# Attention in plain fp32 on part tiles of the array instead of three-way splits, with a new plan

## The chip, the cores and the metric

The kernel runs on one core of a Trainium2 chip. The metric is device microseconds of one execution; lower is better. The engines are TensorE (PE, with its weight loads shown apart as PEld), VectorE (DVE), ScalarE (ACT), GpSimd (POOL) and SyncE (SP), which issues most DMAs.

## The reference

Block attention, then a mixture of experts (two of eight per token), then a gated two-layer network. The change lies in the attention alone, with `q`, `k`, `v` of 4 batches, 8 heads, 576 tokens and 64 features in fp32:

```python
block = 64
scores = (1.0 / np.sqrt(D)) * np.matmul(q, k.transpose(0, 1, 3, 2))
mask = block_i >= block_j                  # a block of 64 queries sees its own and earlier blocks
scores = np.where(mask, scores, -1000000000.0)
scores = scores - np.max(scores, axis=-1, keepdims=True)
attn = np.exp(scores)
attn = attn / (np.sum(attn, axis=-1, keepdims=True) + 1e-09)
attn_out = np.matmul(attn, v)
```

The result, 2304 tokens by 512, is the input of the experts.

## The kernel before

The attention goes through 16 pairs of heads (4 batches, 4 pairs each). `q` and `k` arrive with the features of two heads on the 128 partitions; a query block `i` (of 9, `NB`) needs the keys of blocks 0 to `i`, so `L = 64 (i + 1)` columns. For a pair the stages are: scores (L789), row maximum on DVE (L797), exponential with row sum on ACT (L803), transposes of the 128x128 parts of P on PE (L815), copies out of PSUM (L686), P times V (L847), a closing matmul with `iw` (L871), which is an identity with the router's columns beside it, so that it turns the result back and forms router logits at once, and a scaling by the inverse row sums (L878).

Matmuls are done in three parts of a reduced fp32 format (`F32R`): each operand is split into a high part (a rounding copy) and a low part (the rest), and high x high, high x low and low x high are added up in PSUM. The splits are `hi` and `lo` for V (POOL L749), `q_hi` and `q_lo` (L686, L762), `k_hi` and `k_lo` (L690, L772), and `pt_hi` and `pt_lo` for P (L686, L836). The scores of both heads come from one matmul: `qd` holds a query block of both heads in block-diagonal form, 128x128 with zeros off the diagonal. PV uses a stationary tile of V's high and low part side by side (128 columns), one head at a time. The closing matmul and the transposes run in plain fp32. After each batch three small matmuls with `half` (L894 to L896) add the logits of the two heads.

PSUM has 8 banks: five for transposes, PV and closing results (`tb`), and three for the scores (`sb`, of one and of two).

The order of all this is set by a planner, `Plan`. Each operation is added with the engines that can run it and their costs, with what it depends on, and with a priority; the planner goes through time and, on each free engine, starts the ready operation with the lowest number. `PR` holds the priorities, `TURN` the planner's charge for a change of kind on PE, `STICK` its preference to stay with a kind, `SLACK` how long it waits for the first engine of a choice. The instructions are then issued in that order. DMAs that bring `q`, `k`, `v` of the next pairs and four pairs of expert weights (`RAWP`) are operations of SP in the same plan. Behind the attention come a second plan for the start of the first expert, with tokens known before the last batch is routed, and then written-out loops for the experts and the last network.

Of the kernel before, what the change touches and what calls it, by code (L numbers as in the profile page):

```python
# [7 lines left out]
F32 = mybir.dt.float32  # L8
# [6 lines left out]
OP = mybir.AluOpType  # L15
# [18 lines left out]
SLACK = 0.58  # L34
# [5 lines left out]
STICK = 2.77  # L40
TURN = {(a, b): t for b, r in {"S": {"T": 0.045, "V": 0.083, "F": 0.086, None: 0.084}, "V": {"T": 0.134, "S": 0.072, "F": 0.086, None: 0.09},
                               "T": {"V": 0.038}}.items() for a, t in r.items()}
# [4 lines left out]
PR = {'last': -75, 'ranks': 30, 'rows': -100.0, 'hold': 0.1, 'na': 185.6, 'nb': 352.4, 'lsel': (0, 0, 0, 0, 0, 0, 0, 1, 0, 0), 'f1': (1.7, 24.4, 76.4, 3.2, -11.4, -24.0, -70.7, 4.7), 'f2': (49.7, 0.7, 5.8, 6.0, 38.9, 4.0, 76.2, -1.1), 'fa': (31.8, 1.5, 49.4, -13.5), 'fb': (-32.0, -64.8, 88.3, 44.5), 'fh': (-0.9, 2.5, -24.8, -10.3, 69.9, -36.6, 9.5, -21.3), 'fl': (-24.5, 48.5, -15.0, -13.5, -2.8, 11.5, -62.3, -104.3), 'v': -317.22, 'qk': -13.33, 'keep': 1, 'S': -2.19, 'max': -82.24, 'exp': -40.31, 'pt': 0.29, 'hi': 360.75, 'lo': -37.22, 'hid': True, 'av': 7.35, 'o': 252.33, 'od': True, 'inv': 36.95, 'fin': 28.78, 'x': -1.53, 'route': -0.9, 'rp': 1, 'route2': 6.36, 'xt': -459.1, 'eg': 587.2, 'ex': 432.13, 'ew': 2149.25, 'first': 0, 'sel': 2, 'vh': 3, 'wl': 1, 'wa': -452.8, 'wb': 26.5, 'h': -53.9, 's2': -24.9, 'vs': (-0.62, -2.53, 0.92, 0.17, 0.59, -5.66), 'vpt': (28.74, 8.73, -37.77, -2.51, -5.17, 6.9, -0.23, 1.96), 'vp': (-2.81, -6.08), 'vf': (15.46, 3.5)}  # L47
# [139 lines left out]
def kernel(  # L187
# [49 lines left out]
    FIRST = ((0, 4 * BLK), (4 * BLK, S))  # L237
# [23 lines left out]
    qd = [[raw_p.tile([128, NB, 2, BLK], F32R, name=f"qd{i}{w}") for w in "hl"] for i in range(2)]  # L261

    def zero_qd(e, i):
        for t in qd[i]:
            for h in range(2):
                e.memset(t[64 * h:64 * h + 64, :, 1 - h].bitcast(F32), 0.0)

    zero_qd(nc.vector, 0)
# [15 lines left out]
    FW = D + 4 * E  # L284
    iw = raw_p.tile([128, NP2, FW], F32, name="iw")

    def setup():
        zero_qd(nc.vector, 1)
        for r in range(2):
            rows = slice(r * 64, (r + 1) * 64)  # L290
            nc.vector.tensor_copy(iw[rows, :, 0:D], ident[rows, None, r * 64:(r + 1) * 64].to_broadcast([64, NP2, D]))
# [373 lines left out]
    with actx:  # L665
        pool = lambda name, bufs: actx.enter_context(tc.tile_pool(name=name, bufs=bufs))
        one = pool("one", 1)
        sp_p = pool("split", 3)
        qk_p = pool("qk", 2)
        sm_p = pool("sm", 10)  # L670
        ps_p = actx.enter_context(tc.tile_pool(name="ps_p", bufs=1, space=PSUM))
# [6 lines left out]

        UN = ((0, 1, 3), (2, 4), (5,), (6,), (7,), (8,))
        NU = len(UN)  # L680
        NPAIR = len(pairs)
        BW = 5 * 128
        PART = ((0, 4), (4, NB))
# [3 lines left out]

        def scale(e, o, i):
            if e == "ACT":
                nc.scalar.mul(o, i, qscale)  # L690
            else:
                nc.vector.tensor_scalar(o, i, qscale, None, op0=OP.mult)
# [10 lines left out]
        def first_dve(n):  # L703
            return {"DVE": 0.07 + n / 960.0, "ACT": 0.05 + n / 1200.0}

        def dve(n):
            return {"DVE": 0.07 + n / 960.0}

# [4 lines left out]
        nc.gpsimd.memset(eps, 1.0e-9)  # L713
        P = []
        for i in range(NB):
            P.append(one.tile([128, (i // 2 + 1) * 128], F32, name=f"P{i}"))
            if i % 2 == 0:
                nc.gpsimd.memset(P[i][:, (i + 1) * BLK:], 0.0)
        rs = [one.tile([128, NB], F32, name=f"rs{i}") for i in range(3)]
        pt = [[one.tile([128, 4, 2, 128], F32R, name=f"pt{w}0"), one.tile([128, 5, 5, 128], F32R, name=f"pt{w}1")]  # L720
              for w in "hl"]
        half = one.tile([128, 192], F32, name="half")
        nc.gpsimd.memset(half, 0.0)
        for r in range(2):
            nc.gpsimd.tensor_copy(half[r * 64:(r + 1) * 64, 64:128], ident[r * 64:(r + 1) * 64, r * 64:(r + 1) * 64])
        lgp = [one.tile([128, NB, 2 * E], F32, name=f"lgp{i}") for i in range(2)]

        def init_iw(e):
            for r in range(2):
                rows = slice(r * 64, (r + 1) * 64)  # L730
                for i in range(2):
                    for j, src in enumerate((w_gate, w_noise)):
                        o = D + i * 2 * E + j * E
                        nc.sync.dma_start(iw[rows, :, o:o + E], src.rearrange("(j i d) e -> i d j e", d=D, i=2)[i])
# [4 lines left out]
        sp, kt, oT, ri, xt = {}, {}, {}, {}, {}  # L739

        def hi(e, p):
            t = sp_p.tile([128, NC * 2, 2, D], F32R, tag="v", name="sp_v")
            copy(e, t[:, :, 0], raw["v", p % 2].rearrange("p c h d -> p (c h) d"))
            sp[p] = t

        def lo(e, p):
            t = sp[p]
            r = raw["v", p % 2].rearrange("p c h d -> p (c h) d")
            engine(e).tensor_tensor(t[:, :, 1], r, t[:, :, 0].bitcast(F32), op=OP.subtract)  # L749
            sp[p] = t.rearrange("p (c h) w d -> p c h (w d)", h=2)  # L750

        def rows(t, r, c):
            return t[r, c[0]:c[1]].rearrange("p (i s) -> p i s", s=BLK)

        def q_hi(e, p, h, c=(0, S)):
            r = slice(64 * h, 64 * h + 64)
            copy(e, qd[p % 2][0][r, c[0] // BLK:c[1] // BLK, h], rows(raw["q", p % 2], r, c))

        def q_lo(e, p, h, c=(0, S)):
            r = slice(64 * h, 64 * h + 64)  # L760
            i = slice(c[0] // BLK, c[1] // BLK)
            engine(e).tensor_tensor(qd[p % 2][1][r, i, h], rows(raw["q", p % 2], r, c),  # L762
                                    qd[p % 2][0][r, i, h].bitcast(F32), op=OP.subtract)

        def k_hi(e, p, c=(0, S)):
            if p not in kt:
                kt[p] = [qk_p.tile([128, S], F32R, tag=nm, name=nm) for nm in ("kh", "kl")]
            scale(e, kt[p][0][:, c[0]:c[1]], raw["k", p % 2][:, c[0]:c[1]])

        def k_lo(e, p, c=(0, S)):  # L770
            sl = slice(*c)
            nc.vector.scalar_tensor_tensor(kt[p][1][:, sl], raw["k", p % 2][:, sl], qscale, kt[p][0][:, sl].bitcast(F32),  # L772
                                           op0=OP.mult, op1=OP.subtract)

        views = {}

        def scores(p, u):
            ps = sb[u % 2]
            o = 0
            qh, ql = [t.rearrange("p i h s -> p i (h s)") for t in qd[p % 2]]  # L780
            kh, kl = kt[p]
            for i in UN[u]:
                L = (i + 1) * BLK
                nh = 1 if L <= 512 else 2
                hl = L // nh
                for half_ in range(nh):
                    ks_ = slice(half_ * hl, (half_ + 1) * hl)
                    for a, (w, x) in enumerate(((qh, kh), (qh, kl), (ql, kh))):
                        nc.tensor.matmul(ps[:, half_, o:o + hl], lhsT=w[:, i], rhs=x[:, ks_], start=(a == 0), stop=(a == 2))  # L789
                views[p, i] = ps[:, 0, o:o + hl] if nh == 1 else ps[:, :, :hl]  # L790
                o += hl
# [3 lines left out]
        def rowmax(p, i):  # L795
            nm = sm_p.tile([128, 1], F32, tag="nm", name="nm")
            nc.vector.tensor_reduce(nm, views[p, i], axis=AX.X if i < NB - 1 else AX.XY, op=OP.max, negate=True)  # L797
            nms[p, i] = nm

        def expo(p, i):  # L800
            L = (i + 1) * BLK
            o = P[i][:, :L] if i < NB - 1 else P[i][:, :L].rearrange("p (a l) -> p a l", a=2)
            nc.scalar.activation(o, views.pop((p, i)), AF.Exp, bias=nms.pop((p, i)), scale=1.0,  # L803
                                 accum_out=rs[p % 3][:, i:i + 1])

# [6 lines left out]
        def ptrans(g, n):  # L812
            ps = tb[g.bank]
            for m, (i, c) in enumerate(PT[n]):
                nc.tensor.transpose(ps[:, m * 128:(m + 1) * 128], P[i][:, c * 128:(c + 1) * 128], ident)  # L815

        def pslice(w, n):
            i0, c0 = PT[n][0]
            i1, c1 = PT[n][-1]
            if i1 < 4:  # L820
                return pt[w][0][:, i0:i1 + 1, c0:c1 + 1]
            return pt[w][1][:, i0 - 4, c0:c1 + 1]

        def pview(g, n):
            i0, c0 = PT[n][0]
# [790 lines left out]
```

## Time and profile before

| | |
|---|---|
| median of 3 runs | 1065.29 us (1065.21 to 1066.15) |
| the profiled execution | 1067.7 us, of which its span is 1065.9 us |
| PE busy | 1052.2 us, 99% of the span |
| DVE, ACT, POOL busy | 775.7, 593.3, 319.2 us |
| attention's matmuls | from 5.09 to 227.69 us |
| granted clock, mean | 0.994 |

A matmul's time in the trace is from its start to the modelled end of its result, so successive matmuls overlap in the trace; how often one can start is read from the starts. `128*128` in a row is the size of the stationary tile, `128x320` that of the moving one. A plain fp32 instruction stands in the trace as two records.

### The profile page before, as it was taken

To read this page: it belongs to the slowest core of one execution; us is meant where nothing else is said; L and a number is where in the kernel's file an instruction comes from. 1 tells how busy PE (TensorE), PEld (TensorE's weight loads), DVE (VectorE), ACT (ScalarE), POOL (GpSimd) and SP (SyncE) were. 2 spreads that over 40 slices of the span, in tenths; PEclk is the share of its full clock that TensorE was granted. 3 is DMA by queue.
4 is the path that set the end of the run, shared out by engine and by line. 5 is a ranking of instruction groups with operands and counts; after the bars stand their busy time and mean duration, and the time that the engine had idled before them with its cause. 6 is when DMAs were issued, how large, how long until landed. Compare 5 with 4: busy or idle time off the path is not lost. (4 is left out here: it accounts for less than half of the span.)

```text
span 1065.9 us, 16930 instructions
## 1 busy us (share of the span) xinstructions
PE 1052.2 (99%) x6069; PEld 924.7 (87%) x6069; DVE 775.7 (73%) x1469; ACT 593.3 (56%) x1121; POOL 319.2 (30%) x380
## 2 busy tenths in 40 slices
PE   8999999999999999999999999999999999999998
PEld 6999999988888999999888898988888888888886
DVE  8878787877688889988787866775745755665442
ACT  5777777764456655656555535664535444454442
POOL 6558787624101121202020002743401411310000
PEclk8999999999999999999999999999999999999999
DMA  7534432024999999987978425222202211201001
GB/s 186 147 97 126 132 87 60 16 52 134 323 289 330 281 302 306 264 243 232 218 235 216 155 69 200 78 60 60 60 1 70 51 40 49 60 10 40 1 1 40
DMA packets 163573, 141.80 MB, mean 133 GB/s; under 512 B 92373, under 2 KB 131381, under 8 KB 163485
## 3 DMA queue, kind: packets, MB, share of 16 engines
q1 hardware_dynamic: 147501, 102.79, 35.1%
q0 software_dynamic: 8640, 28.32, 8.9%
q10 hardware_dynamic: 7344, 9.57, 2.7%
q8 instruction: 49, 0.80, 0.3%
q14 instruction: 39, 0.32, 0.1%
HBM read 92.94 MB, written 36.70 MB: 122 GB/s over the span
## 5 line engine op out<-in xcount | busy, mean ns | idle before, releaser
L464 PE MATMUL h<-xh,wah 128*128 128x512 f32 (+8 forms) x832 | 273.3, 328 | 0.7 <-ACT xh L435 0.7
L465 PE MATMUL h<-xl,wah 128*128 128x512 f32 (+8 forms) x832 | 271.9, 327 | 0.4 <-DVE xl L440 0.3
L466 PE MATMUL h<-xh,wal 128*128 128x512 f32 (+8 forms) x832 | 272.0, 327 | 0.0
L1168 PE MATMUL y<-wbl,hh 128*128 128x512 f32 (+1 forms) x576 | 225.7, 392 | 0.1
L1167 PE MATMUL y<-wbh,hh 128*128 128x512 f32 (+1 forms) x576 | 225.6, 392 | 0.1
L1169 PE MATMUL y<-wbh,hl 128*128 128x512 f32 (+1 forms) x576 | 225.0, 391 | 0.0
L464 PEld LDWEIGHTS h<-xh,wah 128*128 128x128 f32 x832 | 156.8, 189 | 16.0 <-ACT xh L435 0.9
L465 PEld LDWEIGHTS h<-xl,wah 128*128 128x128 f32 x832 | 157.0, 189 | 15.5 <-DVE xl L440 0.9
L466 PEld LDWEIGHTS h<-xh,wal 128*128 128x128 f32 x832 | 156.9, 189 | 11.5
L1169 PEld LDWEIGHTS y<-wbh,hl 128*128 128x128 f32 (+1 forms) x576 | 107.3, 186 | 24.7
L487 ACT ACTIVATE hh<-h 128x288 fp32r<-128x288 f32 (+7 forms) x128 | 53.1, 417 | 131.5 <-PE h L466 130.8
L1168 PEld LDWEIGHTS y<-wbl,hh 128*128 128x128 f32 (+1 forms) x576 | 107.4, 186 | 21.4 <-POOL wbl L419 0.8
L1167 PEld LDWEIGHTS y<-wbh,hh 128*128 128x128 f32 (+1 forms) x576 | 107.4, 186 | 21.2 <-issue 0.6
L1530 DVE SCALAR_TENSOR_TENSOR r<-r,h 128x512 f32<-128x512 f32 (+1 forms) x80 | 50.5, 631 | 97.9 <-ACT r L1529 97.6
L1529 ACT ACTIVATE r<-h,three 128x512 f32<-128x512 f32 (+1 forms) x80 | 51.7, 646 | 118.8 <-PE h L466 118.8
L419 DVE TENSOR_TENSOR wal<-wa,wah 128x1024 fp32r<-128x1024 f32 x80 | 106.2, 1328 | 11.8 <-ACT wah L415 10.8
L419 DVE TENSOR_TENSOR wbl<-wb,wbh 128x1024 fp32r<-128x1024 f32 x75 | 101.3, 1350 | 14.8 <-ACT wbh L415 14.6
L415 ACT CAST wbh<-wb 128x1024 fp32r<-128x1024 f32 x80 | 83.9, 1048 | 24.5 <-PE y L1169 14.5
L1532 ACT CAST hh<-r 128x512 fp32r<-128x512 f32 (+1 forms) x80 | 46.2, 577 | 86.0 <-DVE r L1530 86.0
L1533 DVE TENSOR_TENSOR hl<-r,hh 128x512 fp32r<-128x512 f32 (+1 forms) x80 | 56.4, 705 | 51.5 <-ACT hh L1532 51.5
L803 ACT ACTIVATE P<-sb,nm 128x192 f32<-128x192 f32 (+4 forms) x144 | 74.8, 529 | 28.8 <-DVE nm L797 28.8
L415 ACT CAST wah<-wa 128x1024 fp32r<-128x1024 f32 x80 | 83.7, 1046 | 3.9 <-PE h L465 2.4
(269 smaller groups left out, 1785.9 us busy)
## 6 DMA issues: line engine op xcount, KB each, us to landing
wa<-in_moe_w_dram SPq DMA_DIRECT2D x23, 512.0 KB, 4.9
wb<-in_moe_w_dram SPq DMA_DIRECT2D x23, 512.0 KB, 5.6
y_tab<-yo SPq DMA_DIRECT2D x32, 256.0 KB, 4.8
w<-in_moe_w_in_dram SPq DMA_DIRECT2D x16, 512.0 KB, 5.2
y_tab<-zero SPq DMA_DIRECT2D x8, 1024.0 KB, 9.2
w<-in_moe_w_out_dram SPq DMA_DIRECT2D x16, 512.0 KB, 5.6
x_tok<-x SPq DMA_DIRECT2D x32, 144.0 KB, 2.6
wa<-in_moe_w_dram ACTq DMA_DIRECT2D x9, 512.0 KB, 6.3
```

The source lines that it names most:

```text
L415: nc.scalar.copy(w_s[which, u][0], raws[PS[u]][which])
L419: (nc.gpsimd if e == "POOL" else nc.vector).tensor_tensor(lo, raws[PS[u]][which], hi.bitcast(F32), op=OP.subtract)
L464: nc.tensor.matmul(ps, lhsT=wh, rhs=xh, start=first, stop=False)
L465: nc.tensor.matmul(ps, lhsT=wh, rhs=xl, start=False, stop=False)
L466: nc.tensor.matmul(ps, lhsT=wl, rhs=xh, start=False, stop=last)
L487: nc.scalar.activation(h[0][:, c0:c1], ps[:, :c1 - c0], AF.Relu)
L803: nc.scalar.activation(o, views.pop((p, i)), AF.Exp, bias=nms.pop((p, i)), scale=1.0, accum_out=rs[p % 3][:, i:i + 1])
L1167: nc.tensor.matmul(yps[t][:n], lhsT=hh[:, sl], rhs=wh[:, f % 2], start=first, stop=False)
L1168: nc.tensor.matmul(yps[t][:n], lhsT=hh[:, sl], rhs=wl[:, f % 2], start=False, stop=False)
L1169: nc.tensor.matmul(yps[t][:n], lhsT=hl[:, sl], rhs=wh[:, f % 2], start=False, stop=last)
L1529: nc.scalar.activation(r[:, :n], ps[:, :n], AF.Relu, bias=three, scale=1.0)
L1533: nc.vector.tensor_tensor(hl[:, :n], r[:, :n], hh[:, :n].bitcast(F32), op=OP.subtract)
```

## The change

Scores, PV and the closing matmul become plain fp32 matmuls, and the splits of `q`, `k`, `P` and `V` go; only `q` is scaled once (`q_scale`, POOL). Scores are done for each head by itself with 64 partitions and 64 columns of the array: of an odd block and of block 0 head 0 uses the first half of rows and of columns and head 1 the second half of both, and of the other even blocks the columns are exchanged (`flip`). PV and the closing matmul use 128 rows and 64 columns, head 0 (or token half 0) in the first half of the columns. The closing result comes out in token order, so router logits of both heads lie on the same partitions and are added on POOL; the matmuls with `half` go. Scores take four banks, transposes and the rest four. The scores of a pair are three units instead of six: blocks 0 to 4, 5 and 6, 7 and 8. All priorities of the attention's plan are new.

```diff
-SLACK = 0.58
+SLACK = 0.13684749096082838
-STICK = 2.77
+STICK = 3.1977009815403736
+TURN = {(a, b): 0.155 if a and b else 0.09 for a in ("S", "T", "V", None) for b in ("S", "T", "V", None) if a != b}
-        NTB = 5
+        NTB = 4
-        sb = [ps_p.tile([128, i + 1, 512], F32, name=f"sb{i}") for i in range(2)]
+        sb = [ps_p.tile([128, n, 512], F32, name=f"sb{i}") for i, n in enumerate((2, 2))]
-        UN = ((0, 1, 3), (2, 4), (5,), (6,), (7,), (8,))
+        UN = ((0, 1, 2, 3, 4), (5, 6), (7, 8))
+        SAT = {0: (0, 0, 0), 1: (0, 0, 64), 3: (0, 0, 192), 2: (0, 1, 0), 4: (0, 1, 192), 5: (1, 0, 0), 6: (1, 1, 0),
+               7: (1, 0, 0), 8: (0, 0, 0)}
+        ORDER = ((0, 2, 1, 3, 4), (5, 6), (7, 8))
+        SPOOL = ("s0", "s1", "s0")
+        SCOST = (0.87, 0.77, 0.98)
-        PART = ((0, 4), (4, NB))
+        PART = ((0, 5), (5, NB))
+        TPART = ((0, 3), (3, NC))
+        def flip(i):
+            return int(i > 0 and i % 2 == 0)
...
+        def sview(i):
+            t, n, o = SAT[i]
+            L = (i + 1) * BLK
+            return sb[t][:, n, o:o + L] if i < NB - 1 else sb[t][:, 0:2, 0:L // 2]
         def scores(p, u):
-            for i in UN[u]:
+            q_, k_ = qs[p % 2], raw["k", p % 2]
+            for i in ORDER[u]:
...
-                    for a, (w, x) in enumerate(((qh, kh), (qh, kl), (ql, kh))):
-                        nc.tensor.matmul(ps[:, half_, o:o + hl], lhsT=w[:, i], rhs=x[:, ks_], start=(a == 0), stop=(a == 2))
+                for m in range(nh):
+                    for h in range(2):
+                        r = slice(64 * h, 64 * h + 64)
+                        g = h ^ flip(i)
+                        o = sview(i)[64 * g:64 * g + 64]
+                        nc.tensor.matmul(o if nh == 1 else o[:, m], lhsT=q_[r, i * BLK:(i + 1) * BLK],
+                                         rhs=k_[r, m * w:(m + 1) * w], start=True, stop=True)
...
-        def av(g, p, h, part):
+        def av(g, p, part):
...
+            todo = [(c, r) for c in range(last + 1) for r in runs(max(i0, 2 * c), i1)]
+            for n, (c, (a, b)) in enumerate(todo):
+                for h in range(2):
...
+                    nc.tensor.matmul(o[64 * h:64 * h + 64, (a - i0) * BLK:(b - i0) * BLK], lhsT=vs[:, c, h], rhs=x,
+                                     start=(n == 0), stop=(n == len(todo) - 1), skip_group_check=True)
...
         def fin(g, p, part):
-            for i in range(i1 - i0):
-                nc.tensor.matmul(f[:, i], lhsT=oT[p, part][:, i].rearrange("p h s -> p (h s)"), rhs=iw[:, p % NP2],
-                                 start=True, stop=True)
+            for c in range(*TPART[part]):
+                for r in range(2):
+                    i = 2 * c - 1 + r if c else 0
+                    x = oT[p, part][:, (i - i0) * BLK:(i - i0 + 1) * BLK] if c or not r else none
+                    nc.tensor.matmul(f[64 * r:64 * r + 64, c - TPART[part][0]].rearrange("p h w -> p (h w)"), lhsT=x, rhs=w,
+                                     start=True, stop=True)
...
-                k["S", p, u] = add({"PE": sum(s_cost(i) for i in UN[u])}, lambda e, p=p, u=u: scores(p, u),
-                                   ready, U + PR["S"], take=g, kind="S")
+                k["S", p, u] = add({"PE": SCOST[u]}, lambda e, p=p, u=u: scores(p, u),
+                                   ready[0] + (ready[-1] if u else []) + ([k["E", p, 5]] if u == 2 else [k.get(("E", p - 1, 7))] if u == 1 else []), U + PR["S"], take=g, kind="S",
+                                   after=LAND[min(u, 1)] + 0.1 if p == 0 else 0.0)
```

On PE, the scores of three small blocks of a pair before: for each block high x high, low x high and high x low (`kh`, `kl` are the parts of k, `qd1h`, `qd1l` those of q), on the whole array.

```order
L789 MATMUL sb_173<-kh,qd1h 128x64
L789 MATMUL sb_173<-kl,qd1h 128x64
L789 MATMUL sb_173<-kh,qd1l 128x64
L789 MATMUL sb_173<-kh,qd1h 128x128
L789 MATMUL sb_173<-kl,qd1h 128x128
L789 MATMUL sb_173<-kh,qd1l 128x128
L789 MATMUL sb_173<-kh,qd1h 128x256
L789 MATMUL sb_173<-kl,qd1h 128x256
L789 MATMUL sb_173<-kh,qd1l 128x256
```

The same place in the changed program: seven blocks of a pair in one run, and the transposes behind them. `x2` is one matmul for each head.

```order
L752 MATMUL sb_164<-raw_k_77,qs_87 64x64 x2
L752 MATMUL sb_164<-raw_k_77,qs_87 64x192 x2
L752 MATMUL sb_164<-raw_k_77,qs_87 64x128 x2
L752 MATMUL sb_164<-raw_k_77,qs_87 64x256 x2
L752 MATMUL sb_164<-raw_k_77,qs_87 64x320 x2
L752 MATMUL sb_165<-raw_k_77,qs_87 64x384 x2
L752 MATMUL sb_165<-raw_k_77,qs_87 64x448 x2
L777 MATMUL tb_160<-ident,P_0_196 128x128
```

Three matmuls a block for both heads have become two, one a head, and two units of scores stand together.

On PE, the end of the large PV part of one head and the small parts of both heads before (`pth`, `ptl` are the parts of the transposed P).

```order
L847 MATMUL tb_172<-pth_197,sp_v 128x192
L847 MATMUL tb_172<-ptl_199,sp_v 64x192
L847 MATMUL tb_172<-ptl_199,sp_v 64x64
L847 MATMUL tb_172<-pth_197,sp_v 128x64
L847 MATMUL tb_168<-pth_196,sp_v 128x256
L847 MATMUL tb_168<-ptl_198,sp_v 128x256
L847 MATMUL tb_168<-ptl_198,sp_v 64x128
L847 MATMUL tb_168<-pth_196,sp_v 128x128
```

The changed program from the closing matmuls of one part over the large PV part of the next pair to the last scores and the transposes behind.

```order
L857 MATMUL tb_162<-iw,oT_696 64x160
L857 MATMUL tb_162<-iw,none 64x160
L857 MATMUL tb_162<-iw,oT_696 64x160 x4
L822 MATMUL tb_160<-pt_867,raw_v_72 64x256 x6
L822 MATMUL tb_160<-pt_867,raw_v_72 64x64 x2
L822 MATMUL tb_160<-pt_867,raw_v_72 64x128 x2
...
L752 MATMUL sb_165<-raw_k_77,qs_87 64x512 x2
L752 MATMUL sb_164<-raw_k_77,qs_87 64x288 x4
L777 MATMUL tb_161<-ident,P_1_185 128x128 x3
```

Both heads of PV now stand in one run with one bank, and PE goes from column halves to quadrants to the whole array within these rows.

On ACT, one pair before, from the exponentials of blocks 2 and 4 to those of 0, 1 and 3, with copies of P's high part between them.

```order
L803 ACTIVATE P_182,rs_194<-sb_174,nm 128x192
L803 ACTIVATE P_185,rs_194<-sb_174,nm 128x320
L686 CAST pth_197<-tb_168 128x512
L803 ACTIVATE P_179,rs_194<-sb_173,nm 128x64
L803 ACTIVATE P_181,rs_194<-sb_173,nm 128x128
L803 ACTIVATE P_184,rs_194<-sb_173,nm 128x256
L686 CAST pth_196<-tb_171 128x2x128
```

The same place in the changed program: the exponentials of the five small blocks (`P_0_184` is block 4) with the copies of the transposed P of other blocks between them.

```order
L766 ACTIVATE P_0_172,rs_200<-sb_164,nm 128x64
L766 ACTIVATE P_0_176,rs_200<-sb_164,nm 128x128
L685 COPY pt_1023<-tb_160 128x128
L766 ACTIVATE P_0_178,rs_200<-sb_164,nm 128x192
L766 ACTIVATE P_0_182,rs_200<-sb_164,nm 128x256
L685 COPY pt_1023<-tb_163 128x512
L685 COPY pt_1136<-tb_162 128x2x128
L766 ACTIVATE P_0_184,rs_200<-sb_164,nm 128x320
L766 ACTIVATE P_0_188,rs_200<-sb_165,nm 128x384
```

All five share the banks of `sb_164`, which the scores of block 8 take next.

## Rows read from the trace of the kernel before

**Rows 1.** The page: span, busy time of each engine, and slices.

```profile
span 1065.9 us, 16930 instructions
...
PE 1052.2 (99%) x6069; PEld 924.7 (87%) x6069; DVE 775.7 (73%) x1469; ACT 593.3 (56%) x1121; POOL 319.2 (30%) x380
...
PE   8999999999999999999999999999999999999998
...
PEclk8999999999999999999999999999999999999999
```

**Rows 2.** Stages: length, busy PE, PEld, DVE, ACT, POOL, clock, DMA, GB/s.

```profile
12.00:25.00 13.00, 11.45 (x58) 10.47 (x59) 11.61 (x23) 7.92 (x24) 10.59 (x12) 0.61 0.61 154
...
38.00:51.00 13.00, 13.00 (x106) 12.58 (x104) 10.77 (x24) 10.20 (x32) 6.88 (x7) 1.00 0.55 153
...
90.00:103.00 13.00, 12.75 (x106) 12.30 (x105) 11.94 (x44) 9.81 (x32) 8.64 (x15) 1.00 0.47 130
```

**Rows 3.** PE in order of time (start, length), at the attention's two ends.

```profile
5.09 0.38 PE L789 MATMUL sb<-kh,qd0h 128*128 128x64 f32 x1
...
30.74 0.45 PE L789 MATMUL sb<-kh,qd1h 128*128 128x448 f32 x1
...
215.67 0.45 PE L789 MATMUL sb<-kh,qd1h 128*128 128x448 f32 x1
...
225.62 2.23 PE L871 MATMUL tb<-iw,oT 128*128 128x96 f32 x18
227.69 0.60 PE L432 MATMUL tb<-ident,raw_q 128*128 128x128 f32 x4
...
230.10 0.36 PE L464 MATMUL h<-xh,wah 128*128 128x256 f32 x1
```

**Rows 4.** PE in order of time, within one pair.

```profile
104.02 0.44 PE L789 MATMUL sb<-kh,qd1h 128*128 128x384 f32 x1 [0.25 <-ACT P L803]
...
104.65 0.31 PE L847 MATMUL tb<-pth,sp_v 128*128 128x320 f32 x1
104.80 0.31 PE L847 MATMUL tb<-ptl,sp_v 128*128 128x320 f32 x1
...
108.09 0.52 PE L815 MATMUL tb<-ident,P 128*128 128x128 f32 x3
...
109.75 1.15 PE L815 MATMUL tb<-ident,P 128*128 128x128 f32 x9
110.74 1.25 PE L871 MATMUL tb<-iw,oT 128*128 128x96 f32 x10
111.83 0.52 PE L623 MATMUL tb<-rid,sel 128*128 128x80 bf16 x10
```

**Rows 5.** Groups of PE and PEld by line: count, busy us, mean ns.

```profile
L871 PE MATMUL tb<-iw,oT 128*128 128x96 f32 x288 | 36.6, 273 | 0.0
...
L871 PEld LDWEIGHTS tb<-iw,oT 128*128 128x128 f32 x280 | 33.6, 192 | 0.1
...
L847 PEld LDWEIGHTS tb<-ptl,sp_v 128*64 128x64 f32 x94 | 11.2, 135 | 0.0
```

**Rows 6.** ACT in order of time, same pair.

```profile
104.93 0.74 ACT L803 ACTIVATE P<-sb,nm 128x576 f32<-128x576 f32 x1 [0.71 <-DVE nm L797]
...
105.67 0.57 ACT L803 ACTIVATE P<-sb,nm 128x384 f32<-128x384 f32 x1
...
106.22 0.42 ACT L686 COPY oT<-tb 128x320 f32<-128x320 f32 x1
...
107.67 0.48 ACT L686 CAST pth<-tb 128x384 fp32r<-128x384 f32 x1
108.04 0.67 ACT L686 COPY oT<-tb 128x256 f32<-128x256 f32 x2
```

**Rows 7.** DVE in order of time, same pair (the first row a 448 and a 512).

```profile
109.69 1.21 DVE L797 TENSOR_REDUCE nm<-sb 128x1 f32<-128x448 f32 x2
...
112.03 0.66 DVE L878 TENSOR_TENSOR x<-tb,ri 128x480 f32<-128x480 f32 x1 [0.47 <-PE tb L871]
```

More of the change, by code (lines that the diff above doesn't have):

```diff
@@ L260 @@
     NB = S // BLK
[L261 to L268, printed above, removed]
+    qs = [raw_p.tile([128, S], F32, name=f"qs{i}") for i in range(2)]
     ident = const.tile([128, 128], F32, name="ident")
@@ L730, in init_iw @@
                 rows = slice(r * 64, (r + 1) * 64)
[L731 to L734, printed above, removed]
+                for j, src in enumerate((w_gate, w_noise)):
+                    nc.sync.dma_start(iw[rows, :, r, D + j * E:D + (j + 1) * E],
+                                      src.rearrange("(j i d) e -> i d j e", d=D, i=2)[r])
@@ L839, in av, with runs @@
+        def runs(i0, i1):
+            r = []
+            i = i0
+            while i < i1:
+                n = i + 2 if i % 2 and i + 1 < i1 else i + 1
+                if r and i % 2 and n - i == 2 and r[-1][0] % 2 and r[-1][1] - r[-1][0] >= 2:
+                    r[-1] = (r[-1][0], n)
+                else:
+                    r.append((i, n))
+                i = n
+            return r
+        def av(g, p, part):
             i0, i1 = PART[part]
-            vs = sp[p]
-            o = tb[g.bank][:, 0:(i1 - i0) * BLK].rearrange("p (i s) -> p i s", s=BLK)
+            vs = raw["v", p % 2]
+            t = pt[p, part]
+            o = tb[g.bank]
@@ L842, in av @@
             last = (i1 - 1) // 2
-            for c in range(last + 1):
-                a = max(i0, 2 * c)
-                for w in ((0, 1) if c < last else (1, 0)):
-                    n = 2 * D if w == 0 or (i1 - a) * BLK >= 256 else D
-                    nc.tensor.matmul(o[:n, a - i0:], lhsT=vs[:, c, h, :n], rhs=pt[w][part][:, a - i0:, c, h * BLK:(h + 1) * BLK],
-                                     start=(c == 0 and w == 0), stop=(c == last and w == 0))
-        def av_out(e, g, p, h, part):
+            todo = [(c, r) for c in range(last + 1) for r in runs(max(i0, 2 * c), i1)]
@@ L891, in lgm @@
-        def lgm(g, b):
-            o = tb[g.bank][:, 0:NC * 2 * E].rearrange("p (c e) -> p c e", c=NC)
-            t = lgp[b % 2]
-            nc.tensor.matmul(o[:, 0], lhsT=half[:, 64:], rhs=t[:, 0], start=True, stop=True)
-            nc.tensor.matmul(o[:, 1:], lhsT=half[:, 64:], rhs=t[:, 1::2], start=True, stop=False)
-            nc.tensor.matmul(o[:, 1:], lhsT=half[:, 0:128], rhs=t[:, 2::2], start=False, stop=True)
-        def lg_out(e, g, b):
-            copy(e, lg[b % 2], tb[g.bank][:, 0:NC * 2 * E].rearrange("p (c e) -> p c e", c=NC))
+            t = [xt[p][:, :, h, D:] for h in range(2)]
```

291 lines of the change are left out of this document (120 added, 171 removed).

## The prediction

> **What bounds the kernel now.** I read the page first: TensorE (PE) is busy 99% of the span and shows tens in nearly every slice, while VectorE (DVE), ScalarE (ACT) and GpSimd (POOL) are well below [rows 1]. The table by stages shows that this holds inside the attention stage too: 13.00 of 13 us at 38 to 51, 12.75 at 90 to 103, with ACT near 10 and DVE at 11 to 12, and the granted clock at its full level (1.00) from 25 us on; only at 12 to 25, when the first pair still waits for its operands, is it at 0.61 [rows 2]. So a microsecond taken from PE in the attention stage is a microsecond of the end, as long as no other engine comes to the fore. The stage runs from the first score matmul at 5.09 to the identity matmuls' end at 227.69, and the first expert's matmuls begin at 230.10 [rows 3]. The 448-column score of pair 1 starts at 30.74 and that of pair 15 at 215.67: 184.93 us for 14 pairs, 13.21 us a pair [rows 3]; 16 of them are 211.4 and the rest of the stage's 222.6, 11.2 us, is start and end.
>
> Where the 13.21 go is read from one pair's matmuls in order of time, by starts [rows 4]: P and V from 104.65 to 108.09, 3.44 us; the closing identity matmuls 0.109 a record (110.74 to 111.83 for 10), 18 records, 1.96; transposes of P 0.11 each (nine from 109.75 to 110.74), 25 of them, 2.75; the scores take the rest, some 5 us, with a wait of 0.25 for ScalarE's exponentials; and 0.35 us of routing matmuls fall in one pair of four.
>
> **The change, part by part.** Kept: the 25 transposes, 2.75. Gone: 30 score, 28 PV and 18 identity records with their 128-wide loads. In their place stand plain fp32 matmuls whose columns are counted from the code and the order: scores 2880 columns (64 to 576 in steps of 64) for each of two heads, 5760; PV 576 + 1024 for each head, 3200; ten identity matmuls of 160, 1600.
>
> What a column of plain fp32 costs, the trace doesn't show, for the only such matmuls are narrow. It gives bounds: the identity matmul is fp32 and stands as two records an instruction (288 records for 144) [rows 5], 0.109 us each for 96 columns [rows 4], which a 128-wide load would explain by itself; if it were the columns, it would be 1.14 ns a column and record, 2.27 an instruction. From below, a record can't go faster than the three-way split's, 0.15 us for 320 columns (104.65 to 104.80) [rows 4], 0.46 ns, so 0.92 an instruction. I take 1.67 ns, a little above the middle of 1.6, because it is four whole cycles of the 2.4 GHz level. One after another this is 9.6 for scores, 5.3 for PV, 2.7 for identity: 17.6 us where 10.4 stood. So everything hangs on how many matmuls run side by side. The code lays them out for it: score matmuls on four quadrants of 64x64 (odd blocks straight, even blocks crossed), PV and identity on two column halves. No row shows two matmuls side by side, so the bounds are one and four (two). I take the full overlap: 9.6/4 + 5.3/2 + 2.7/2 = 6.4 us. The loads don't forbid it: a 64-wide load is 135 ns where a 128-wide one is 192 [rows 5], so at most 0.11 - 0.057 = 0.054 us in the stream, and 104 records a pair make 5.6 even if no two loads overlap.
>
> Changes of shape are new. In the steady state the order goes through seven a pair: scores, transposes, identity and PV, scores, transposes, identity and PV, transposes. What one costs is between nothing and an emptied array; the row for that is a matmul's length less its spacing, 0.31 - 0.15 [rows 4], 0.16 us. I take that: 1.15 us a pair. The Trainium skill (TensorEngine Tiling, Key Properties) says that a change of tiling mode, not of tile, drains TensorE; by that rule it is the 0.16, and without it the seven would cost up to 1.15 us less, 18 us over the stage.
>
> The sum a pair: 2.75 + 6.4 + 1.15 + 0.1 of routing + 0.4 of waits (the 0.25 above and a bit for four transposing banks instead of five) = 10.8, so 2.4 less than 13.2; 16 pairs, 38 us.
>
> The other engines must fit in 10.8. ScalarE: an exponential of 576 columns holds it 0.74 and one of 384 0.55 (104.93 to 105.67, and so on to the copy at 106.22) [rows 6], about 0.17 + 0.99 ns a column: nine take 4.4; a copy of 384 takes 0.37 (107.67 to 108.04) [rows 6], and by the order ScalarE keeps some 3100 columns of copies a pair, 3.0: 7.4 together. VectorE: maxima 3.6 (1.21 us for 960 columns [rows 7], 2880 of them), the scaled results 1.1 (0.66 for 480 [rows 7], 800 of them), four small reciprocals and one copy of 512 in most pairs about 1.2: 6. Both lose work (the low parts of P, the casts of k and V, half of the output copies), and GpSimd, busy 6.9 to 8.6 us of 13 [rows 2], loses the splits of q and V; all this was hidden behind PE and gives nothing by itself. The last logits' matmuls go, under 1 us at the end. The start keeps its 11 us: the wait for the first exponentials and the half clock stay, though scores begin earlier without splits.
>
> Behind the stage nothing changes in form: the 836 us from 230.10 on are PE's, and the weights that the stage prefetches are asked for in the same pairs.
>
> The profiled execution took 1067.7 us for its span of 1065.9; less 38 it is 1029.5, and the median of the runs lies 2.4 below it: **1027 us**.
>
> **Rivals.**
> *Overlap of scores by two only.* Records of one instruction need the same quadrant and matmuls start in program order in every row of the trace, so the second record may hold back the next head; or the two heads of a block, which come from two row halves and write one bank, may not run at once. Then scores take 4.8: 13.2 a pair, no gain, about 1065, within 6 of it either way. For it: no row shows side by side work; against it: the load of the next weights already runs under a matmul (PE 99% with PEld 87% [rows 1]). The Trainium skill (TensorEngine Tiling, Gotcha 1) says that different row tiles cannot access one PSUM bank at a time; by that rule the time would be this rival's 1065. No row here shows it, and it gets most of this rival's chance.
> *No overlap, the slower case.* If plain fp32 matmuls on part tiles run one after another: 2.75 + 17.6 + 1.15 + 0.5 = 22 a pair, 8.8 more, 140 us: about 1205. It decides at a mean overlap of 17.6 / (13.2 - 4.4) = 2.0; below that the kernel is slower.
> *The score banks or ScalarE bound.* The last two blocks wait for the first five's exponentials, and these for the eighth block of the pair before: 0.8 of scores, 2.2 of exponentials, 1 of scores, two maxima of 1.3, an exponential of 0.74 and four hand-overs of 0.17 each are 6.7 of 10.8, if nothing is in front on ScalarE and VectorE. Each of some ten steps that finds a copy of 0.4 in front adds to it; from 10.8 on this chain decides. At 11.9 a pair: 1045.
>
> **How the numbers follow.** Chances: full overlap 0.62; the bank chain 0.11; overlap by two 0.16 (half of it with less than no gain); none 0.11. Full overlap alone: 1014 (a change of shape at half its price and 1.5 ns a column) to 1042 (1.67 and 0.9 us of waits more); with 2.27 ns it would be 1064. The range goes from 1014 into the second rival, to 1066, and leaves out the dear cases and the far low end, some 2 in 10. A measurement here tells 0.2%, 2.1 us, from no change. Faster: the first two cases and a bit of the third, 0.77; same 0.04; slower 0.19.
>
> **What would show it.** Right: scores of the first seven blocks of a pair (14 instructions) within some 1.6 us, starts of different quadrants closer than a record is long; 10.5 to 11 us from pair to pair; PE still at 95% or more, ACT near 7.5 of 10.8; the first expert's matmuls near 192 instead of 230. Wrong: score records that start only when the record before ends; PE waiting for L766's exponentials before each score group; a granted clock below 1.00 in the stage, since then every term doubles; or a tail behind the stage longer than 836 us.

## The result and the profile after

The changed kernel takes 1041.44 us (median of 4 runs, 1040.44 to 1041.77), the kernel before 1065.72 beside it: a ratio of 0.9768, 95% interval 0.9751 to 0.9785. 24 us came where 38 were forecast; the time lies inside the range, 14 us above the number.

The page (span, busy time, the clock of 40 slices) answers to [rows 1]:

```profile
span 1040.0 us, 17400 instructions
...
PE 1008.0 (97%) x6493; PEld 841.7 (81%) x6493; DVE 708.2 (68%) x1354; ACT 563.0 (54%) x1043; POOL 247.0 (24%) x335
...
PEclk9999999999999999999999999999999999999999
```

The table of stages (columns as in [rows 2]):

```profile
12.00:25.00 13.00, 12.27 (x141) 8.29 (x139) 8.85 (x27) 9.16 (x33) 1.85 (x2) 1.00 0.27 65
38.00:51.00 13.00, 12.29 (x157) 8.67 (x156) 7.57 (x22) 7.76 (x20) 4.11 (x6) 1.00 0.77 205
90.00:103.00 13.00, 11.84 (x144) 8.57 (x144) 7.35 (x22) 8.64 (x29) 5.42 (x11) 1.00 0.41 93
```

PE is no longer full in the attention: 11.84 of 13 us at 90 to 103, where it was 12.75. PE in order of time, at the stage's ends and through one pair (`x28` and `x12` are records of the scores of the first seven and the last two blocks, two for an instruction; times of two rows overlap, so lengths are read from start to start):

```profile
4.27 1.96 PE L752 MATMUL sb<-raw_k,qs 64*64 64x64 f32 x28 [0.24 <-DVE qs L734]
...
25.89 1.20 PE L752 MATMUL sb<-raw_k,qs 64*64 64x512 f32 x12
...
100.67 1.85 PE L752 MATMUL sb<-raw_k,qs 64*64 64x64 f32 x28
102.45 0.87 PE L777 MATMUL tb<-ident,P 128*128 128x128 f32 x6
103.74 0.33 PE L777 MATMUL tb<-ident,P 128*128 128x128 f32 x1 [0.42 <-ACT P L766]
104.00 0.35 PE L857 MATMUL tb<-iw,oT 128*64 128x160 f32 x1
...
105.78 1.97 PE L822 MATMUL tb<-pt,raw_v 128*64 128x256 f32 x24 [0.75 <-ACT pt L685]
108.20 1.20 PE L752 MATMUL sb<-raw_k,qs 64*64 64x512 f32 x12 [0.46 <-ACT P L766]
109.34 1.75 PE L777 MATMUL tb<-ident,P 128*128 128x128 f32 x14
111.01 0.76 PE L857 MATMUL tb<-iw,oT 128*64 128x160 f32 x8
111.61 1.17 PE L822 MATMUL tb<-pt,raw_v 128*64 128x64 f32 x20
112.71 0.66 PE L777 MATMUL tb<-ident,P 128*128 128x128 f32 x4
113.29 1.85 PE L752 MATMUL sb<-raw_k,qs 64*64 64x64 f32 x28
...
196.74 1.20 PE L752 MATMUL sb<-raw_k,qs 64*64 64x512 f32 x12 [0.46 <-ACT P L766]
...
208.60 0.36 PE L456 MATMUL h<-xh,wah 128*128 128x256 f32 x1 [1.05 <-DVE xl L432]
```

Pairs 1 to 15 are (196.74 - 25.89) / 14 = 12.20 us apart, where 13.21 stood [rows 3] and 10.8 was forecast; the pair shown takes 12.62, with 1.63 us of waits in brackets. The span is 25.9 us shorter: 14.1 in these 14 pairs; 4.9 ahead of them (30.74 in [rows 3] against 25.89; the clock, 0.61 at 12 to 25 before [rows 2], is now 1.00); 2.6 between pair 15 and the first expert's matmuls (14.43 before, 11.86 now); 4.4 behind that (831.4 us from there to the end, 835.8 before). These are two single executions, and the one of the kernel before had a mean granted clock of 0.994; two other executions of it, at 1.000, had spans of 1062.7 and 1063.4 us instead of 1065.9, so as far as these tell the clock is at most about 3 us of the 25.9.

ScalarE and VectorE in that pair (their rows answer to [rows 6, 7]):

```profile
102.40 0.31 ACT L766 ACTIVATE P<-sb,nm 128x64 f32<-128x64 f32 x1 [1.03 <-DVE nm L759]
...
103.23 0.37 ACT L766 ACTIVATE P<-sb,nm 128x128 f32<-128x128 f32 x1 [0.42 <-DVE nm L759]
...
104.57 0.42 ACT L766 ACTIVATE P<-sb,nm 128x192 f32<-128x192 f32 x1 [0.89 <-DVE nm L759]
...
104.98 1.02 ACT L685 COPY pt<-tb 128x128 f32<-128x128 f32 x3
```

```profile
101.88 0.42 DVE L759 TENSOR_REDUCE nm<-sb 128x1 f32<-128x64 f32 x2 [0.75 <-PE sb L752]
102.83 0.36 DVE L759 TENSOR_REDUCE nm<-sb 128x1 f32<-128x192 f32 x1 [0.53 <-ACT P L766]
103.72 1.82 DVE L759 TENSOR_REDUCE nm<-sb 128x1 f32<-128x256 f32 x4 [0.52 <-ACT P L766]
```

Here is what is new: an exponential waits for a maximum, and a maximum waits for an exponential, in turns. No maximum needs an exponential's result. The maximum of block 2 (192 columns) starts only after the exponential of block 0, though block 2's scores ended at 101.22. So the third exponential starts at 104.57, the copies behind it on ScalarE at 104.98, and V's matmuls, which need one of these copies, at 105.78. Groups of PE by line from 26 to 190 us (some 13 of the 16 pairs; "the stretch" from here on), with the idle time ahead of each:

```profile
L777 PE MATMUL tb<-ident,P 128*128 128x128 f32 x332 | 48.4, 282 | 5.1 <-ACT P L766 4.0 <-ACT pt L685 1.0
L752 PE MATMUL sb<-raw_k,qs 64*64 64x288 f32 (+8 forms) x527 | 41.1, 415 | 3.6 <-ACT P L766 3.6
L822 PE MATMUL tb<-pt,raw_v 128*64 128x64 f32 (+2 forms) x572 | 40.6, 291 | 8.8 <-ACT pt L685 8.8
```

That is 17.5 us of waits for ScalarE. The waits of ScalarE and VectorE for one another in the stretch (us in total, times, longest):

```profile
ACT P L766 <- DVE nm L759: 28.7, 36, 1.8
...
DVE nm L759 <- ACT P L766: 13.4, 25, 0.6
```

The second kind did not appear among the waits read before.

**Theories.** A: PE's work in a pair is as forecast (10.4 us), and the waits, put at 0.4, are some 2; they come from exponentials that start late since maxima and exponentials of blocks in one score buffer take turns. B: the overlap or the changes of shape cost more than forecast, and the waits only fill time that PE would need anyhow.

### The profile page after: what moved, and what is told of

It reads as the page before. It is cut to its first block, busy times and chain, and to the rows that moved or that the text cites. A ratio compares the mean times of both kernels' runs of the same rounds, so it can differ in the third digit from the quotient of the medians.

```text
span 1040.0 us, 17400 instructions
## 1 busy us (share of the span) xinstructions
PE 1008.0 (97%) x6493; PEld 841.7 (81%) x6493; DVE 708.2 (68%) x1354; ACT 563.0 (54%) x1043; POOL 247.0 (24%) x335
## 5 line engine op out<-in xcount | busy, mean ns | idle before, releaser
L411 DVE TENSOR_TENSOR wal<-wa,wah 128x1024 fp32r<-128x1024 f32 x80 | 106.3, 1328 | 13.6 <-ACT wah L407 12.5
L759 DVE TENSOR_REDUCE nm<-sb 128x1 f32<-128x448 f32 (+4 forms) x144 | 63.3, 486 | 59.9 <-PE sb L752 32.6
L766 ACT ACTIVATE P<-sb,nm 128x448 f32<-128x448 f32 (+4 forms) x144 | 75.9, 541 | 38.2 <-DVE nm L759 38.2
```

Source lines behind the costliest of these rows:

```text
L411: (nc.gpsimd if e == "POOL" else nc.vector).tensor_tensor(lo, raws[PS[u]][which], hi.bitcast(F32), op=OP.subtract)
L759: nc.vector.tensor_reduce(nm, sview(i), axis=AX.X if i < NB - 1 else AX.XY, op=OP.max, negate=True)
L766: nc.scalar.activation(o, sview(i), AF.Exp, bias=nms.pop((p, i)), scale=1.0, accum_out=rs[p % 3][:, COL[i]:COL[i] + 1])
```

## The experiments

The kernel before, run beside them, had medians of 1065.5 to 1065.9 us.

**1. All maxima of unit 0 first.** The order on every engine stays; only the maxima's place among the exponentials, and with it the waits, changes.

```diff
-            nm = sm_p.tile([128, 1], F32, tag="nm", name="nm")
-            nc.vector.tensor_reduce(nm, sview(i), axis=..., op=OP.max, negate=True)
-            nms[p, i] = nm
+            if (p, i) in nms:
+                return
+            for x in (UN[0] if i in UN[0] else (i,)):
+                nm = sm_p.tile([128, 1], F32, tag="nm", name="nm")
+                nc.vector.tensor_reduce(nm, sview(x), axis=..., op=OP.max, negate=True)
+                nms[p, x] = nm
```

> The changed kernel with one thing moved: the row maxima of blocks 0 to 4 of a pair are written down together, before the first exponential of these blocks. Every engine keeps its instructions in the same order; what goes is the wait of a maximum for the exponential of another block in the same score bank, and back. Theory A (the gain is short because VectorE's maxima and ScalarE's exponentials take turns on the score banks, which lengthens the way from scores to P, for which PE then waits): from pair to pair 12.6 falls by 0.8 to 1.4 us, the kernel by 12 to 20 us, to 1021 to 1029, and PE's idle time before L777, L822 and L752, 16 us in the stage, falls to less than 6. Theory B (ScalarE's own work and four transposing banks make the waits): the exponentials begin a little later and nothing is gained, 1038 to 1044. Theory C (PE's own work with the changes of shape is longer than computed): as B.

Measured: 1036.1 us (1035.5 to 1037.67), ratio 0.9725, interval 0.9709 to 0.9741: 5 us gained. V's waits fall from 8.8 to 1.9 us, but the transposes' rise from 5.1 to 7.2: the first exponential now waits for all five maxima.

```profile
101.24 0.32 ACT L769 ACTIVATE P<-sb,nm 128x64 f32<-128x64 f32 x1 [2.03 <-DVE nm L762]
```

Theory A expected 12 to 20 us and less than 6 us of waits; 5 us came, and 12.5 us of waits are left. The turns cost time, but this cure has its own price.

**2. No exchange of quadrants.** Each head keeps one quadrant for all blocks, so only two of four are used; the halves of the even blocks' P are exchanged between the heads and the output's with them.

```diff
-                        g = h ^ flip(i)
+                        g = h
```

> The changed kernel with the scores of all blocks on the two quadrants of the diagonal (the column halves are not exchanged for blocks 2, 4, 6, 8, so the halves of P of these blocks belong to the other head than the following stages take them for). Instructions, order and counts stay. If four quadrants work side by side in the changed kernel: the run of 28 score records takes 3.0 to 3.2 us where it takes 1.78, that of 12 records 1.9 to 2.1 where it takes 1.14, 2.1 us more on PE a pair, of which the waits of 1.6 hide a part: 1050 to 1075. If only two records ever run at a time (the second record of an instruction holds the next): no change in the runs of records, 1041.

Measured: 1067.14 us (1066.23 to 1068.94), ratio 1.0012, interval 1.0002 to 1.0023. PE in order of time:

```profile
113.79 3.24 PE L752 MATMUL sb<-raw_k,qs 64*64 64x64 f32 x28
116.96 0.98 PE L777 MATMUL tb<-ident,P 128*128 128x128 f32 x7
...
122.08 2.04 PE L752 MATMUL sb<-raw_k,qs 64*64 64x512 f32 x12 [0.46 <-ACT P L766]
124.06 1.75 PE L777 MATMUL tb<-ident,P 128*128 128x128 f32 x14
```

The first seven blocks take 3.17 us instead of 1.78, the last two 1.98 instead of 1.14: four quadrants do work side by side, and the gain hangs on it. The first seven blocks have 1792 columns a quadrant here and 960 in the fuller quadrant of the changed kernel, so 832 columns cost 3.17 - 1.78 = 1.39 us, 1.67 ns each; 1792 of them are 2.99, and 0.18 is left for the turn.

**3. Two more changes of shape ahead of each group of transposes,** and **4.** the same added matmul without a change of shape.

```diff
+            nc.tensor.matmul(ps[0:64, 0:8], lhsT=ident[0:64, 0:64], rhs=ident[0:64, 0:8], start=True, stop=True)   # 3
+            nc.tensor.matmul(ps[:, 0:8], lhsT=ident, rhs=ident[:, 0:8], start=True, stop=True)                     # 4
```

> The changed kernel with one more matmul ahead of each of the eight groups of transposes of a pair: 64x64, 8 columns, plain fp32, its result overwritten by the transposes. It adds two changes of shape to a group that stands between other transposes. At 0.16 us a change and 0.11 for the two records a group becomes 0.4 us longer: a run of 14 transposes in four groups of 1.67 us becomes 3.1 to 3.4. If changes of shape are nearly free (0.05), it becomes 2.2 to 2.5. The kernel: 10 to 50 us longer in the first case, under 15 in the second.

> As the run with 64x64, but the added matmul has the shape of the transposes, 128x128, 8 columns, so that no change of shape is added, and its two loads are twice as wide (0.11 each): a group becomes 0.22 us longer, a run of 14 transposes in four groups 2.5 to 2.6 us. If the run with 64x64 is longer than this one, it is by the change of shape.

Measured: 1058.88 and 1054.0 us, one run each. The fourteen transposes in four groups take 2.97 us with the change (102.97 to 105.94) and 2.43 without (101.61 to 104.04). One group in the third kernel, then in the fourth, PE in order of time:

```profile
103.67 0.28 PE L776 MATMUL tb<-ident 64*64 64x8 f32 x2
103.88 0.66 PE L778 MATMUL tb<-ident,P 128*128 128x128 f32 x4
104.46 0.28 PE L776 MATMUL tb<-ident 64*64 64x8 f32 x2
```

```profile
102.21 0.29 PE L776 MATMUL tb<-ident 128*128 128x8 f32 x2
102.36 0.64 PE L778 MATMUL tb<-ident,P 128*128 128x128 f32 x4
102.83 0.29 PE L776 MATMUL tb<-ident 128*128 128x8 f32 x2
```

A group takes 0.79 us against 0.62. The small matmul without a change stands for 0.15; on 64 columns its two records take about 0.11, an estimate from the spacing of 0.054 that the prediction worked out for a 64-wide load, so two changes cost 0.79 - 0.47 less 0.11 to 0.15, which is 0.09 to 0.11 each; in the changed kernel's pair it is 0.14 (four transposes from 112.71 to 113.29 take 0.58, of which 0.44 are theirs). The 2.97 lies between the two ranges expected (3.1 to 3.4 and 2.2 to 2.5), the 2.43 just under its own. 0.16 was taken, so the missing 1.4 us a pair are not there, and what B says of changes of shape falls.

**5. Order by bank.** Blocks 0, 1, 3 lie in one bank of the score buffer, 2 and 4 in the other.

```diff
-            for x in (UN[0] if i in UN[0] else (i,)):
+            for x in ((0, 1, 3, 2, 4) if i in UN[0] else (i,)):
...
         def expo(p, i):
+            i = {2: 3, 3: 2}.get(i, i)
```

> The five maxima of unit 0 stand together, as in the version that brought 1036.1 us, but in the order 0, 1, 3, 2, 4 (the three blocks of one score bank first, then the two of the other), and the exponentials in that order too; both banks are still one buffer. If VectorE and ScalarE take turns because of the bank, the first exponential starts after three maxima (0.66 us of work) instead of five (1.35 us), PE's waits of 0.64 and 0.44 us a pair fall by up to 0.7 us: about 1026 us (1023 to 1030). If they take turns because the program's semaphores guard the buffer of two banks as a whole, nothing changes: 1036 (1034.5 to 1037.5). I expect the second.

Measured: 1038.34 us (1035.73 to 1039.58), no faster than the first experiment. ScalarE:

```profile
102.95 0.31 ACT L769 ACTIVATE P<-sb,nm 128x64 f32<-128x64 f32 x1 [2.03 <-DVE nm L762]
```

The wait is the 2.03 us of experiment 1 again: it is set by the buffer of two banks as a whole, not by the bank. Experiment 6 keeps this order and splits the buffer, and the wait goes: it is a semaphore of the program, not a stall of the chip. The Trainium skill (PSUM — Partial Sum Buffer, PSUM bank collisions raise a hardware error) says that two engines must not touch the same bank and quadrant at once, reads included, and that software has to guard it. By that rule the first exponential needs three maxima behind it, not five; no run here lets the two engines collide.

**6. Two buffers of one bank,** with that order; **7.** the two buffers alone, with maxima and exponentials woven as in the changed kernel; **8.** the two buffers, and the planner told of the maxima as they are issued.

```diff
-        sb = [... for i, n in enumerate((2, 2))]
+        sb = [... for i, n in enumerate((1, 2, 1))]
-               2: (0, 1, 0), 4: (0, 1, 192), ... 7: (1, 0, 0), 8: (0, 0, 0)}
+               2: (2, 0, 0), 4: (2, 0, 192), ... 7: (0, 0, 0), 8: (1, 0, 0)}
# 8
+                    if i not in (1, 3, 4):
-                    m_ = add({"DVE": 0.07 + L / 960.0}, ...
+                        m_ = add({"DVE": {0: 0.68, 2: 0.67}.get(i, 0.07 + L / 960.0)}, ...
```

In these three the scores of block 8 of one pair of the sixteen are overwritten by the next pair's before its exponential reads them; number and size of the instructions are the same. Experiment 9 guards this too.

> The same order, and the two banks of unit 0 are two buffers of one bank each (blocks 0, 1, 3 and 2, 4; block 7 goes to the first, block 8 to the two banks that blocks 5 and 6 left). TensorE's order is the same row for row. If what is left of the excess is the wait for exponentials that start too late: they start 0.7 us earlier in each pair, the 0.64 us ahead of the transposes of blocks 0 and 1 goes, that ahead of unit 2 falls below 0.2, a pair takes 11.1 to 11.4 us instead of 12.09, and the time is 1025 us (1020 to 1030). Rival: the wait only moves (unit 2's scores now wait for the exponential of block 6 too, 0.57 us more): 1033 to 1037.

> The changed kernel with the two buffers alone, maxima and exponentials woven as the plan puts them. Maxima of blocks 2 and 4 no longer wait for exponentials of the other bank; the maximum of block 3 still does for those of blocks 0 and 1. If turns on one buffer are what the 2.0 us of waits in a pair are made of, about half goes: 1031 us (1026 to 1037). If the turns cost only where several blocks of one bank are woven, it stays near the changed kernel's 1041 (1038 to 1042).

> The two buffers, and the planner told what is emitted: one operation of 0.68 us for the maxima of blocks 0, 1, 3, one of 0.67 us for 2 and 4, exponentials in that order; its costs and priorities are otherwise as they were, so it lays out TensorE's order anew (transposes in more and smaller groups, about two more changes of shape a pair at 0.12 to 0.15 us each). If waits that the plan does not see are the cost, a true plan takes the last of them away: 1026 us (1018 to 1032). If the order that the priorities were found for matters more, it is slower than with the old order: 1030 to 1040.

Measured: 1026.05 us (1025.55 to 1026.54), ratio 0.9625; 1031.33 (1030.57 to 1031.92), ratio 0.9673; 1036.39 (1035.14 to 1037.21), ratio 0.9722. Six and seven came out as theory A has it. They also give blocks 7 and 8 other buffers, which moves a wait rather than ending it: the 3.6 us ahead of the last scores become waits inside their group (its `x12` records are up to 1.87 us long, 1.20 without a wait). In eight the waits are short too (4.3 us in the stretch), but its order breaks the seven blocks' run of scores in every second pair, with V's matmuls between the parts. What makes up its 10 us against six (changes of shape, waits inside groups) was not taken apart.

**9. The same as six with the guard for all pairs,** and **10.** the copy of the transposed blocks 0 and 1 on VectorE.

```diff
# 9
         def scores(p, u):
+            if u == 1 and p and (p - 1, 8) not in early_8:
+                rowmax(p - 1, 8)
+                expo(p - 1, 8)
# 10
         def pt_out(e, g, p, n):
+            e = "DVE" if n == 0 else e
```

> The version with two buffers of one bank again, with one guard more: the scores of blocks 5 and 6 of the third pair may not overwrite those of block 8 of the second pair before its exponential has read them (the earlier one left that out, for this one block of one pair). One pair of sixteen waits for that, by 1 us at most: 1026.5 us (1025 to 1028.5).

> The same, and the copy of the transposed blocks 0 and 1 (0.3 us) goes from ScalarE to VectorE, which stands idle there. In the version before, the scores of block 8 wait inside unit 2 until the exponential of block 6 has read their banks, some 0.47 us a pair (its twelve records take 1.60 us where 1.13 would do); the copy stands ahead of that exponential. If ScalarE's queue is what is late, the exponential comes 0.3 us sooner in 14 pairs: 4 us less, 1022.5 us (1020 to 1024.5). If the wait only moves (to V, for the other copies, or to VectorE's maxima): 1026 to 1028.

Measured: 1026.66 us (1025.27 to 1026.83), ratio 0.9634, interval 0.9621 to 0.9647; and 1025.01 (1024.4 to 1026.8), ratio 0.962, interval 0.9607 to 0.9633. Both beat the changed kernel, by 14.8 and 16.4 us; between the two the 4 us expected shrank to 1.65, less than the intervals tell apart. The traces show why: the `x12` records of the last scores, 1.20 us long without a wait, are 1.66 to 1.79 in six pairs of the ninth and 1.39 to 1.51 in the same pairs of the tenth, 1.7 us in all, and in the other pairs there was little to gain. The ninth's PE, groups by line in the stretch of before, and one pair in order of time:

```profile
L789 PE MATMUL tb<-ident,P 128*128 128x128 f32 x362 | 53.4, 283 | 0.8 <-ACT P L778 0.5
L757 PE MATMUL sb<-raw_k,qs 64*64 64x288 f32 (+8 forms) x544 | 46.8, 417 | 1.0 <-ACT P L778 0.9
L834 PE MATMUL tb<-pt,raw_v 128*64 128x64 f32 (+2 forms) x628 | 45.0, 292 | 0.8 <-ACT pt L685 0.7
```

```profile
99.21 1.94 PE L834 MATMUL tb<-pt,raw_v 128*64 128x256 f32 x24
101.08 1.67 PE L757 MATMUL sb<-raw_k,qs 64*64 64x512 f32 x12
102.67 1.75 PE L789 MATMUL tb<-ident,P 128*128 128x128 f32 x14
...
106.63 1.85 PE L757 MATMUL sb<-raw_k,qs 64*64 64x64 f32 x28
108.41 1.33 PE L789 MATMUL tb<-ident,P 128*128 128x128 f32 x7
```

ScalarE's first exponential of that pair now waits for scores, no longer for a maximum, and the same last scores in the tenth:

```profile
97.28 0.31 ACT L778 ACTIVATE P<-sb,nm 128x64 f32<-128x64 f32 x1 [1.25 <-PE sb L757]
```

```profile
100.49 1.39 PE L757 MATMUL sb<-raw_k,qs 64*64 64x512 f32 x12
```

Idle time falls with the time: from the changed kernel's 17.5 us of waits in the stretch to 12.5 in experiment 1, 7.7 in 7 and 2.6 in 9 are 5.0, 9.8 and 14.9 us less; the times are 5.3, 10.1 and 14.8 less. That they agree so closely is luck, for the stretch leaves out three pairs and the counts leave out waits inside groups; and in experiment 8, with another order, 13.2 us less of waits go with 5.1 us less time. The lengths show it without these gaps: from the last scores of pair 1 to those of pair 15 the changed kernel takes 170.85 us, experiments 1, 7 and 9 take 165.92, 161.03 and 156.95, with TensorE's matmuls in the same order. So the waits were on the path that sets the end, and B falls. The ninth's 11.21 us a pair are still 0.7 above the work of 10.5 (summed up below); in the pair shown this is hidden inside groups: the `x12` from 101.08 takes 1.59 where 1.14 does without a wait (block 8 waits for the exponential of block 6), and the seven transposes from 97.11 take 1.23 where 0.92 would do.

**11. V's matmuls head after head,** in the changed kernel, and **12.** the same once more.

```diff
-            for n, (c, (a, b)) in enumerate(todo):
-                for h in range(2):
+            for h in range(2):
+                for n, (c, (a, b)) in enumerate(todo):
```

> The changed kernel, with V's matmuls in another order: all of one head (columns 0 to 63 of the array), then all of the other, instead of head by head in turn. If matmuls of the two column halves run beside one another only when they stand next to one another, V costs its full 5.3 us a pair instead of 2.65, of which the waits for ScalarE (1.6 to 2.0 us a pair) can take up a part: 24 to 42 us more, 1065 to 1084. If TensorE overlaps them however they stand, or V's two halves never overlapped, no change: 1039 to 1045.

> The same kernel once more, for its trace: the one profiled execution of the run before it took 3641.8 us, with every matmul of the program two to four times as long at a granted clock of 1.0, and nothing can be read from it; its other execution took 1068.8 us. If the halves overlap only head by head in turn: 1068 us (1064 to 1073), the 24 records of V's larger part (1.87 us head by head) 3.2 to 3.7 us, the 20 of the smaller (1.10 us) 1.8 to 2.2. If the disturbance was of this order itself: again far over 1100.

Measured: of the first's two executions the profiled one took 3641.82 us, with every group of matmuls several times as long, and tells nothing; the other took 1068.8; the second took 1067.55 (1066.53 to 1069.17, 10 runs), ratio 1.0016, interval 1.0006 to 1.0026. Its PE in order of time:

```profile
102.77 3.16 PE L822 MATMUL tb<-pt,raw_v 128*64 128x256 f32 x23
105.86 0.53 PE L615 MATMUL tb<-rid,sel 128*128 128x80 bf16 x10
...
109.72 1.88 PE L822 MATMUL tb<-pt,raw_v 128*64 128x64 f32 x20
111.53 0.66 PE L777 MATMUL tb<-ident,P 128*128 128x128 f32 x4
```

V takes 3.09 and 1.81 us (3.2 to 3.7 and 1.8 to 2.2 were expected), where head by head in turn it takes 1.87 (99.21 to 101.08 in the ninth's rows) and 1.10: the column halves overlap only when their matmuls stand next to one another.

## Why the prediction was right, and which term was off

**The bound.** Right: PE's time in the attention was what counted, and everything hung on overlap. Of the prediction's own signs, the short run of the first seven blocks (1.78 us for "some 1.6") and the clock of 1.00 spoke for it. Against it spoke the distance of pairs (12.20 us for 10.5 to 11), the first expert's matmuls (208.6 us for 192) and PE's waits for L766 ahead of the last scores.

**Overlap and price of a column.** Right. Four quadrants and two column halves work side by side, and both are needed: without either the whole gain is gone (experiments 2 and 12). The first rival (overlap of scores by two only) is what experiment 2 was made into, and it measured 1067 where that rival said 1065. The rule of the Trainium skill behind it (TensorEngine Tiling, Gotcha 1) does not hold here in the form stated: the two heads of a block come from two row halves and write two partition halves of one bank, and seven blocks of them take 1.78 us, no longer than four quadrants allow. In the changed kernel's trace the records of block 6 of both heads start at 101.60 and end at 102.14. The scores of a pair came to 2.56 us without turns (1.60 and 0.96) instead of 2.4, since the exchange fills the quadrants unevenly: of the first seven blocks 2, 4 and 6 have 960 columns, 0, 1, 3 and 5 have 832.

**Changes of shape.** Right in size: 0.09 to 0.18 us at the places read, where 0.16 was taken.

**PE's work in a pair.** By start to start, with each group's waits left out: scores 1.78 + 1.14, transposes 0.92 + 1.67 + 0.58, closing matmuls 0.87 + 0.60, V 1.87 + 1.10: 10.5 us, turns included, without routing matmuls (about 0.1 a pair). 10.4, with routing, was the sum without waits.

**Waits.** This is the term that was mis-sized: "+ 0.4 of waits (the 0.25 above and a bit for four transposing banks instead of five)". In the pair shown 12.62 - 10.5 = 2.1, on average 12.20 - 10.5 = 1.7 us. The prediction took the wait of the old order over into the new one. It had looked at the score banks as a rival, but as a chain of lengths (6.7 of 10.8 us); what cost time was that the new layout puts five blocks into one buffer that two engines read, so that maxima and exponentials of different blocks exclude one another, and that the transposes of blocks 0 and 1 stand in PE's queue with the closing matmuls and V behind them. That rival's 11.9 us a pair and its mechanism, one engine waiting for the other on a score buffer, were nearest to what happened; its place was another. The time alone does not tell them apart: 1041.44 lies beside this rival's 1045 and at the far end of full overlap, 1042, for which the prediction allowed 0.9 us of waits more.

**Start, end and the stage behind.** Forecast at no change. The start, though, gained 4.9 us, 0.8 of it because the first scores start at 4.27 instead of 5.09; the end of the attention gained 2.6, and the stage behind 4.4. The prediction kept the half clock at the start, and there is none now; by the executions at 1.000 that is worth at most about 3 us, and what makes up the rest was not tested. The 4.4 all come late: up to 732 us before and 711 after the stage takes as long in both (502.0 and 502.7 us), and behind that the 128x512 matmuls of L464 to L466 take 394 to 395 ns before and 389 after, at a granted clock of 1.00 in both. Why stays open. These 12 us, which nothing forecast, are luck: without them the mis-sized term would have shown in full, for 16 pairs gave 16 us, not 38.

**The range.** Its lower end, 1014, is a slip: half the price of a turn (0.57) and 1.5 ns a column (0.65) are 1.2 us a pair, 20 us less than 1027, about 1007. So is 1.15 for seven turns of 0.16, which is 1.12. Neither bears on the outcome.

**ScalarE and VectorE.** Right in the main: busy 7.8 to 8.6 and 7.4 to 7.6 of 13 us in the stages at 38 and 90, which is 7.3 to 8.1 and 6.9 to 7.1 in a pair of 12.2, where 7.4 and 6 were counted; neither is the bound by its sum.

## What to carry to other kernels

When blocks are packed into fewer PSUM buffers, read in the order which engines share a buffer: here the guard works by buffer, and an engine with idle time to spare can still be late in each block. A sum of busy times can't show this; a row in which an engine waits for one that needs nothing of it does. And here small tiles paid only while their neighbours in the queue used other parts of the array: the order of issue is half of the layout.

## What the runs showed of the hardware

- Matmuls of different heads on opposite quadrants, and on the two column halves, run side by side: 28 score records 1.78 us with four quadrants, 3.17 with two.
- Side by side a plain fp32 column costs 1.67 ns (1792 columns a quadrant in 3.17 us, 960 in 1.78). One after another it costs less: V's 2048 columns in 3.09 us are 1.51 ns, its 1152 in 1.81 us 1.57 ns, turns included. So two halves together are 1.65 times as fast as one after the other (3.09 against 1.87 us), not twice.
- The clock at 12 to 25 us was granted at 1.00 with PE busy 12.27 of 13 us; before it was 0.61, and at 8 to 12 PE was busy 2.52 of 4 us there, 3.27 now.
